# Attention and a mixture of experts on Trainium2: the turn of y split into column halves and moved behind the state's update

## The chip, the cores and the metric

The kernel runs on one core of a Trainium2 chip. Time is the device time of one execution in microseconds (us), the median of three runs. The core's engines work side by side: PE (TensorE: products; a product first loads its weights, 128 rows by up to 128 columns, and then streams columns against them), DVE (VectorE), ACT (ScalarE), POOL (GpSimd) and SP (SyncE, which here only starts transfers). Each engine runs its instructions in the order in which they are written, and waits on semaphores for what the others deliver.

## The reference

```python
gamma = 1.0 - 2.0 ** (-5.0 - np.arange(H))             # B, H, S, D = 4, 8, 768, 64
for t in range(S):
    state = gamma[None, :, None, None] * state + np.einsum('bhd,bhe->bhde', k[:, :, t], v[:, :, t])
    y[:, :, t] = np.einsum('bhd,bhde->bhe', q[:, :, t], state) / np.sqrt(D)
x = y.transpose(0, 2, 1, 3).reshape(B * S, H * D)      # 3072 tokens of 512
noisy = x @ w_gate + np.log1p(np.exp(x @ w_noise)) * noise
top2 = np.argpartition(-noisy, 2, axis=1)[:, :2]       # of 8 experts, softmax over the two
for e in range(8):                                     # F = 1024
    h = np.maximum(x[mask] @ w1[e], 0.0)
    out[mask] += top2_w[mask, k, None] * (h @ w2[e])   # for the tokens that chose e
```

## The kernel before

The program has two parts. The first is the attention, in 24 chunks of 128 tokens, six for each batch (chunk j, c = j % 6 within the batch). Here and below, a tile is named as the rows of the trace name it.

For chunk j, `qk(j)` (L353) multiplies keys and scaled queries into two banks `pA` (16 instructions on 64 rows of the array), and DVE masks them with the decay into `am` (L356). `y_state(j)` (L368) adds queries times the state `U` into `pY`; it is left out for c = 0. `y_mm(j)` adds `am` times the scaled values `vp` (L375), has ACT copy `pY` to `yt` (L379), brings the state up to date in `pU` (L384, left out for c = 5; ACT copies it to `U`, L386), and has ACT square `yt` into `sq` (L388). `x_turn(j)` turns `yt` so that tokens lie on partitions: four f32 products against `turn`, an identity with the gates' weights beside it, give both the turned y and the logits, in `pT` (L401); four one-column products over `sq` (L405) give each token's sum of squares. `x_scale(j)` (L420, L421, DVE) makes a power of two of that, and `x_split(j)` writes x as two f16 parts: ACT the first (L427) and the logits `lgs` (L415), DVE the rest (L431), SP the result to `xbuf` in DRAM (L432).

The loop over j issues, in this order: `qk(j+1)`, `x_turn(j-1)`, `y_state(j)`, steps of the routing (which expert takes which token: `middle`, `mid`, `todo`, `first_todo`), `v_scale(j+1)` and `q_scale(j+2)` on POOL (L326, L334, which make `vp` and `qs` out of loaded `in_v` and `in_q`), `x_scale(j-1)`, `load(j+4)`, `x_split(j-1)`, `y_mm(j)`. Sums of squares of the experts' weights (L207, ACT) are among the steps. Before the loop PE multiplies constants (`busy`, L122, `WARM` of them in two portions around the products L129 and L130, and L821 three times).

The second part is the experts. A block f of expert e is `mm1` (L873 to L875: x and w1 in f16 parts, twelve products into a bank `pH`), `h_hi` (ACT, L879, `hh`) and `h_lo` (DVE, L882, `hl`), and then the second layer in L919 to L921 and L975. Behind the loop stand `p0` to `p7`, the first 384 slots of expert 0, which cover the last turn `x_turn(23)`, its x and the last routing: `mb` (L481) is what the product L492 counts with. L217 is a product for the scale of a weight. In the blocks of expert 0 that follow, counted by n, `tables()` runs at n = 11: `ranked` (L666, L668) and `rows_of` (L634 to L636) make on DVE the table `idx`, by which POOL gathers tokens (L723).

Of the kernel before, what the change touches and what calls it, by code (L numbers as in the profile page):

```python
# [10 lines left out]
F32 = mybir.dt.float32  # L11
F16 = mybir.dt.float16
BF = mybir.dt.bfloat16
# [7 lines left out]
C = 128  # L21
# [39 lines left out]
QW = HP * C + NC * HP  # L61
WARM, BUSY = (4, 3), 3

# [38 lines left out]
def moe_kernel(ctx, tc, qT, kT, kt, vt, noise, wgn, w1, w2, ctab, qtab, xbuf, out):  # L102
# [220 lines left out]
    def v_scale(j):  # L323
        c = j % NC
        VP[j] = loads.tile([128, H, D], F32, name="vp", bufs=2)
        nc.gpsimd.tensor_tensor(VP[j], IN["v", j].rearrange("p (h d) -> p h d", h=H),  # L326
                                vtab[:, c, :, None].to_broadcast([128, H, D]), op=OP.mult)
# [43 lines left out]
    def y_mm(j):  # L371
        c = j % NC
        for i in range(HP):
            for s in range(2):
                nc.tensor.matmul(yplace(j, i, s), VP[j][:, 2 * i + s, :], AM[j][:, s, i, :],  # L375
                                 start=(not c and i < 2), stop=True, skip_group_check=True)
        YT[j] = loads.tile([128, 2, 2, C], F32, name="yt", bufs=2)
        y = YT[j].rearrange("p s g c -> p (s g c)")
        nc.scalar.activation(y.rearrange("p (s x) -> p s x", s=2), PY.pop(j)[:, :, :2 * C], AF.Copy)  # L379
        if c < NC - 1:  # L380
            for i in range(HP):
                for s in range(2):
                    h = 2 * i + s
                    nc.tensor.matmul(pU[s * 64:s * 64 + 64, i, :], IN["kt", j][:, h * 64:h * 64 + 64], VP[j][:, h, :],  # L384
                                     start=(c == 0 and i == 0), stop=True, skip_group_check=True)
            nc.scalar.activation(U[(c + 1) % 2], pU, AF.Copy)  # L386
        SQ[j] = loads.tile([128, KT, C], BF, name="sq", bufs=1)
        nc.scalar.activation(SQ[j].rearrange("p n c -> p (n c)"), y, AF.Square)  # L388

    def x_turn(j):  # L390
# [8 lines left out]
        for s in range(2):  # L399
            for g in range(2):  # L400
                nc.tensor.matmul(p[:, s, g * 128:g * 128 + XW], y[:, s, g, :], turn[:, v, 2 * s + g],  # L401
                                 start=(g == 0), stop=True, skip_group_check=True)
        q = SQ.pop(j)
# [255 lines left out]
    def ranked():  # L659
# [8 lines left out]
        nc.vector.tensor_reduce(tk.rearrange("p (r t) -> p r t", r=m), tp, axis=AX.X, op=OP.add)  # L668
        rows_of(tk, NBLK, NCOL)

# [79 lines left out]
    def P(j, f, *a, d=mid):  # L750
        d.setdefault(j, []).append((f, a))
# [36 lines left out]
    P(23, route_p, 1, d=middle)  # L788
    P(23, route_n, 1)
    P(23, route_g, 1)  # L790
    at(0, turn_gate, 0)
# [30 lines left out]
    for j in range(NCH):  # L822
        if j + 1 < NCH:
            qk(j + 1)
        if j:
            x_turn(j - 1)
        y_state(j)
        for f, a in middle.get(j, []):
# [17 lines left out]
        for f, a in todo.get(j, []):  # L846
            f(*a)
        y_mm(j)
        for f, a in first_todo.get(j, []):
# [12 lines left out]
    def mm1_pe(e, n0, n1, f, between=None):  # L862
        MM[0] += 1
        tag = "pA" if MM[0] % 3 else "pX" if MM[0] > 3 else "pU"
        p = (psum2[0] if tag == "pX" else psum).tile([128, 512], F32, name="pH", tag=tag, bufs=2 if tag == "pA" else 1)
# [140 lines left out]
    x_turn(j)  # L1006
    x_scale(j)
    h_hi(*p0)
    h_lo(*p0)
    x_split(j, lambda: route_x(2, 0, NC))  # L1010
    pctx.close()
# [13 lines left out]
    route_c(2)  # L1025
    w_hi(0, "2", 1)
    h_lo(*p1)
    h_lo(*p2)
# [53 lines left out]

    def tables():
        ranked()
        for _ in range(2):
            ahead.pop(0)()

    for e in range(E):
# [10 lines left out]
        for n0, n1 in cols:  # L1099
# [3 lines left out]
            for f in range(FT):  # L1103
# [33 lines left out]
                if e == 0 and n == 11:  # L1137
                    tables()
                if e == 0 and n == 13:
# [139 lines left out]
```

## Time and profile before

| | |
|---|---|
| runs, us | 646.54, 646.7, 647.61 (median 646.7) |
| profiled execution | 645.92, its span 644.1 |
| PE busy | 634.5 us, 99% |
| DVE, ACT, POOL busy | 287.6 (45%), 300.2 (47%), 204.0 us (32%) |
| mean granted TensorE clock | 0.998 |
| DMA | 113 MB, 175 GB/s |

The span runs from the first to the last instruction of the profiled execution; the device time is longer by what lies around it. Busy shares are means over the whole program. The loop over the chunks takes the first 111 us, the experts the rest.

### The profile page before, as it was taken

The page shows a single profiled execution, that of the slowest core. Times are in us where ns is not written, and L with a number is a line of the kernel's source. Part 1 is how long each engine was busy: PE and PEld are TensorE (multiplying, and loading weights), DVE is VectorE, ACT ScalarE, POOL GpSimd, SP SyncE. Part 2 cuts the span into 40 slices and gives each one's busy share as a digit, 9 for nine tenths or more (in the row PEclk, how much of TensorE's full clock was granted, in tenths as well). Part 3 has the DMA queues.
Part 4 walks back from the last instruction along what each step waited for, and adds up shares of the span by engine and source line. Part 5 has one row for each costly group of instructions (what it writes and reads, how often), then busy time and mean ns, then how long its engine had stood idle before and what let it go on. Part 6 is the DMA issues. An engine that isn't in the chain of part 4 may idle for free.

```text
span 644.1 us, 12255 instructions
## 1 busy us (share of the span) xinstructions
PE 634.5 (99%) x4919; PEld 390.3 (61%) x4919; DVE 287.6 (45%) x740; ACT 300.2 (47%) x559; POOL 204.0 (32%) x166
## 2 busy tenths in 40 slices
PE   9999999999999999999999999999999999999995
PEld 6999998549578544554455445544554465455574
DVE  4678785897454221654162226222622262215020
ACT  6577457615652543554354345434543454344121
POOL 4555472041540134104410433043304430430214
PEclk9999999999999999999999999999999999999999
DMA  8999999978888066845773576447654784483303
GB/s 300 379 386 382 335 319 268 371 188 295 167 139 263 4 130 113 235 99 101 148 191 136 91 137 182 162 82 132 192 161 82 120 211 147 86 118 62 50 10 43
DMA packets 94423, 113.02 MB, mean 175 GB/s; under 512 B 60662, under 2 KB 61820, under 8 KB 90780
## 3 DMA queue, kind: packets, MB, share of 16 engines
q1 hardware_dynamic: 82576, 85.57, 44.2%
q0 software_dynamic: 11776, 26.63, 23.4%
q8 instruction: 40, 0.66, 0.4%
q14 instruction: 19, 0.16, 0.1%
q10 hardware_dynamic: 12, 0.01, 0.0%
HBM read 72.66 MB, written 26.42 MB: 154 GB/s over the span
## 4 chain that ended last, share of the span: by engine, by line
PE 95%; ACT 2%; DVE 1%; issue 1%; POOL 0%; DMA 0%; POOLq 0%; ACTq 0%
PE pH L873 13%; PE pH L875 13%; PE pH L874 13%; PE pO L919 12%; PE pO L921 12%; PE pO L920 12%; PE pA L353 4%; PE pT L401 4%; PE pY L375 4%; PE pT L975 2%; PE pY L368 2%; PE pO L963 2%; PE pU L384 1%; ACT junk L207 1%; PE pO L951 1%; PE pO L949 1%
## 5 line engine op out<-in xcount | busy, mean ns | idle before, releaser
L910 POOL DMA_INDIRECT out<-ot,idx x51 | 82.4, 1616 | 323.2 <-ACT ot L905 181.1
L873 PE MATMUL pH<-xe,w1h 128*128 128x384 f16 (+5 forms) x576 | 180.9, 314 | 0.4 <-DVE hl L882 0.4
L875 PE MATMUL pH<-xe,w1l 128*128 128x384 f16 (+5 forms) x576 | 180.8, 314 | 0.0
L874 PE MATMUL pH<-xe,w1h 128*128 128x384 f16 (+5 forms) x576 | 180.8, 314 | 0.0
L882 DVE SCALAR_TENSOR_TENSOR hl<-pH,hh 128x384 f16<-128x384 f32 (+5 forms) x144 | 75.6, 527 | 140.0 <-ACT hh L879 139.5
L921 PE MATMUL pO<-w2h,hl 128*128 128x512 f16 x344 | 130.4, 379 | 0.0
L920 PE MATMUL pO<-w2l,hh 128*128 128x512 f16 x344 | 130.4, 379 | 0.0
L919 PE MATMUL pO<-w2h,hh 128*128 128x512 f16 x344 | 130.3, 379 | 0.0
L879 ACT ACTIVATE hh<-pH 128x384 f16<-128x384 f32 (+5 forms) x144 | 67.3, 467 | 122.5 <-PE pH L875 111.7
L905 ACT ACTIVATE ot<-pO,gse 128x512 f32<-128x512 f32 x45 | 30.9, 687 | 155.7 <-PE pO L921 139.5
L235 DVE SCALAR_TENSOR_TENSOR w1l<-wst,wsc,w1h 128x1024 f16<-128x1024 f32 x28 | 35.9, 1284 | 95.3 <-ACT w1h L230 95.3
L873 PEld LDWEIGHTS <-w1h 128*128 128x128 f16 x576 | 56.3, 98 | 33.0 <-issue 2.7
L875 PEld LDWEIGHTS <-w1l 128*128 128x128 f16 x576 | 56.3, 98 | 30.9
L874 PEld LDWEIGHTS <-w1h 128*128 128x128 f16 x576 | 56.3, 98 | 30.3 <-issue 0.5
L207 ACT ACTIVATE junk<-wst 128x1024 bf16<-128x1024 f32 x64 | 67.2, 1050 | 0.1
L723 POOL DMA_INDIRECT xg<-xbuf,idx x54 | 57.4, 1062 | 29.0 <-issue 11.9
L921 PEld LDWEIGHTS <-hl 128*128 128x128 f16 x344 | 33.6, 98 | 40.6
L919 PEld LDWEIGHTS <-hh 128*128 128x128 f16 x344 | 33.6, 98 | 40.6 <-issue 0.4
L920 PEld LDWEIGHTS <-hh 128*128 128x128 f16 x344 | 33.6, 98 | 39.6
L356 DVE TENSOR_TENSOR am<-pA,mask 128x512 f32<-128x512 f32 x48 | 30.8, 683 | 17.9 <-PE pA L353 17.9
L326 POOL TENSOR_TENSOR vp<-in_v,cs 128x512 f32<-128x512 f32 x24 | 25.2, 1049 | 36.3 <-issue 16.3
L230 ACT ACTIVATE w2h<-wst,wsc 128x1024 f16<-128x1024 f32 x32 | 36.5, 1140 | 0.2 <-DVE wsc L185 0.2
(181 smaller groups left out, 681.3 us busy)
## 6 DMA issues: line engine op xcount, KB each, us to landing
wst<-w SPq DMA_DIRECT2D x28, 1024.0 KB
in_q<-qT SPq DMA_DIRECT2D x24, 256.0 KB
in_k<-kT SPq DMA_DIRECT2D x24, 256.0 KB
in_v<-vt SPq DMA_DIRECT2D x24, 256.0 KB
in_kt<-kt SPq DMA_DIRECT2D x24, 256.0 KB
xbuf<-x SPq DMA_DIRECT2D x24, 256.0 KB
out<-zero SPq DMA_DIRECT2D x6, 1024.0 KB
wst<-w SPq DMA_DIRECT2D x8, 512.0 KB
```

What stands on the lines that cost most here:

```text
L207: nc.scalar.activation(junk, st[:, i * 1024:(i + 1) * 1024], AF.Square, accum_out=ss[:, i:i + 1])
L230: nc.scalar.activation(hi, st[:, i * 1024:(i + 1) * 1024], AF.Copy, scale=sc[:, 0:1])
L723: nc.gpsimd.indirect_dma_start(out=x[:n], out_offset=None, in_=xbuf[:128 + B0 * S] if e == 0 and t < 3 else xbuf, in_offset=bass.IndirectO ...
L873: nc.tensor.matmul(p[:, :n], whi, xh, start=(k == 0), stop=False)
L874: nc.tensor.matmul(p[:, :n], whi, xl, start=False, stop=False)
L875: nc.tensor.matmul(p[:, :n], wlo, xh, start=False, stop=(k == KT - 1))
L879: nc.scalar.activation(hh[:, f, n0:n1], p, AF.Relu)
L882: nc.vector.scalar_tensor_tensor(hl[:, f, n0:n1], p, 0.0, hh[:, f, n0:n1], op0=OP.max, op1=OP.subtract)
L910: nc.gpsimd.indirect_dma_start(out=out, out_offset=bass.IndirectOffsetOnAxis(ap=idx[:n, i:i + 1], axis=0), in_=ot[:n], in_offset=None, com ...
L919: nc.tensor.matmul(p, a, WT["2h"][:, f, :], start=(f == 0), stop=False)
L920: nc.tensor.matmul(p, a, WT["2l"][:, f, :], start=False, stop=False)
L921: nc.tensor.matmul(p, c, WT["2h"][:, f, :], start=False, stop=(f == FT - 1))
```

## The change

Four things change. In `x_turn` each of the four products becomes two, on 64 columns of weights each, that write the two halves of the partitions. In the loop `x_turn(j-1)` moves behind `y_state(j)` and `y_mm(j)`, which both move up, ahead of the steps of routing; `vp` gets a third buffer and `sq` a second. At the start, five and two constant products stand in place of four and three. Behind the loop, `x_split(23)` comes ahead of `h_hi(p0)`, `h_lo(p0)` moves back to the other `h_lo`, the banks of the `pH` tiles are dealt out in another order, `route_n` and `route_g` of the second group go from ahead of `x_split` to behind it in chunk 23, and `tables` is cut in two: `ranked` at n = 11, `rows_of` at n = 12.

```diff
@@ -59,7 +59,7 @@
 CW = _o
 SOON = _C["vtab"][1]
 QW = HP * C + NC * HP
-WARM, BUSY = (4, 3), 3
+WARM, BUSY = (5, 2), 3
 
 
 def _constants():
@@ -322,7 +322,7 @@
 
     def v_scale(j):
         c = j % NC
-        VP[j] = loads.tile([128, H, D], F32, name="vp", bufs=2)
+        VP[j] = loads.tile([128, H, D], F32, name="vp", bufs=3)
         nc.gpsimd.tensor_tensor(VP[j], IN["v", j].rearrange("p (h d) -> p h d", h=H),
                                 vtab[:, c, :, None].to_broadcast([128, H, D]), op=OP.mult)
 
@@ -384,7 +384,7 @@
                     nc.tensor.matmul(pU[s * 64:s * 64 + 64, i, :], IN["kt", j][:, h * 64:h * 64 + 64], VP[j][:, h, :],
                                      start=(c == 0 and i == 0), stop=True, skip_group_check=True)
             nc.scalar.activation(U[(c + 1) % 2], pU, AF.Copy)
-        SQ[j] = loads.tile([128, KT, C], BF, name="sq", bufs=1)
+        SQ[j] = loads.tile([128, KT, C], BF, name="sq", bufs=2)
         nc.scalar.activation(SQ[j].rearrange("p n c -> p (n c)"), y, AF.Square)
 
     def x_turn(j):
@@ -398,8 +398,9 @@
         y = YT.pop(j)
         for s in range(2):
             for g in range(2):
-                nc.tensor.matmul(p[:, s, g * 128:g * 128 + XW], y[:, s, g, :], turn[:, v, 2 * s + g],
-                                 start=(g == 0), stop=True, skip_group_check=True)
+                for r in (slice(0, 64), slice(64, 128)):
+                    nc.tensor.matmul(p[r, s, g * 128:g * 128 + XW], y[:, s, g, r], turn[:, v, 2 * s + g],
+                                     start=(g == 0), stop=True, skip_group_check=True)
         q = SQ.pop(j)
         for n in range(KT):
             nc.tensor.matmul(PT[j, "s"], q[:, n], oneb[:, 0:1], start=(n == 0), stop=(n == KT - 1), skip_group_check=True)
@@ -666,7 +667,7 @@
         nc.vector.tensor_tensor(tp, v[:, None].to_broadcast(s4), pm[:, :, None, :].to_broadcast(s4), op=OP.mult)
         tk = work.tile([128, NCB], F32, name="tk")
         nc.vector.tensor_reduce(tk.rearrange("p (r t) -> p r t", r=m), tp, axis=AX.X, op=OP.add)
-        rows_of(tk, NBLK, NCOL)
+        return tk
 
     def rank_caps():
         m = E - 1
@@ -786,8 +787,8 @@
     P(22, route_m, 1)
     at0(22, route_c, 1)
     P(23, route_p, 1, d=middle)
-    P(23, route_n, 1)
-    P(23, route_g, 1)
+    at(23, route_n, 1)
+    at(23, route_g, 1)
     at(0, turn_gate, 0)
     at(3, turn_ident, 1)
     at(3, turn_gate, 1)
@@ -822,9 +823,10 @@
     for j in range(NCH):
         if j + 1 < NCH:
             qk(j + 1)
+        y_state(j)
+        y_mm(j)
         if j:
             x_turn(j - 1)
-        y_state(j)
         for f, a in middle.get(j, []):
             f(*a)
         if j < 2:
@@ -845,7 +847,6 @@
             x_split(j - 1)
         for f, a in todo.get(j, []):
             f(*a)
-        y_mm(j)
         for f, a in first_todo.get(j, []):
             f(*a)
     lctx.close()
@@ -861,7 +862,7 @@
 
     def mm1_pe(e, n0, n1, f, between=None):
         MM[0] += 1
-        tag = "pA" if MM[0] % 3 else "pX" if MM[0] > 3 else "pU"
+        tag = "pU" if MM[0] == 3 else "pX" if MM[0] > 3 and MM[0] % 3 == 1 else "pA"
         p = (psum2[0] if tag == "pX" else psum).tile([128, 512], F32, name="pH", tag=tag, bufs=2 if tag == "pA" else 1)
         n = n1 - n0
         for k in range(KT):
@@ -1005,9 +1006,8 @@
         zero_out(i)
     x_turn(j)
     x_scale(j)
+    x_split(j, lambda: route_x(2, 0, NC))
     h_hi(*p0)
-    h_lo(*p0)
-    x_split(j, lambda: route_x(2, 0, NC))
     pctx.close()
     psum2.append(ctx.enter_context(tc.tile_pool(name="psum2", bufs=1, space=bass.MemoryType.PSUM)))
     psum2[0].tile([128, DM], F32, name="pO", tag="pY", bufs=2)
@@ -1024,6 +1024,7 @@
     p3 = first(3, lambda: route_p(2))
     route_c(2)
     w_hi(0, "2", 1)
+    h_lo(*p0)
     h_lo(*p1)
     h_lo(*p2)
     h_hi(*p3)
@@ -1080,8 +1081,8 @@
     for t in range(3):
         put(0, t, made[t])
 
-    def tables():
-        ranked()
+    def tables(tk):
+        rows_of(tk, NBLK, NCOL)
         for _ in range(2):
             ahead.pop(0)()
 
@@ -1135,7 +1136,9 @@
                     flush()
                     out_scale(0, 3, NBLK)
                 if e == 0 and n == 11:
-                    tables()
+                    tk = ranked()
+                if e == 0 and n == 12:
+                    tables(tk)
                 if e == 0 and n == 13:
                     ahead.pop(0)()
                 n += 1
```

PE, one turn of the loop before; the names are tiles, `x8` counts what stands in a row:

```order
L368 MATMUL pY<-qs,U_170 64x128 x8
L375 MATMUL pY<-am,vp 64x128 x8
L384 MATMUL pU<-vp,in_kt 64x64 x8
L353 MATMUL pA<-qs,in_k 128x128 x8
L401 MATMUL pT<-turn,yt 128x144 x4
L405 LDWEIGHTS sq
L405 MATMUL pT<-oneb,sq 128x1
```

And PE in the changed kernel, one turn from its qk on:

```order
L353 MATMUL pA<-qs,in_k 128x128 x8
L368 MATMUL pY<-qs,U_171 64x128 x8
L375 MATMUL pY<-am,vp 64x128 x8
L384 MATMUL pU<-vp,in_kt 64x64 x8
L402 MATMUL pT<-turn,yt 64x144 x8
L406 LDWEIGHTS sq
L406 MATMUL pT<-oneb,sq 128x1
```

The turn stands between update and squares instead of between qk and squares, and qk is followed by the state's products. All lines behind L385 have a number one higher in the changed kernel.

DVE behind the loop, from the scale of the last x on, before (`hl` of 128x384 is `h_lo`, first of p0, then of p1 and p2):

```order
L420 TENSOR_SCALAR p2m<-pT 128x1
L421 TENSOR_SCALAR xsa<-p2m 128x1
L882 SCALAR_TENSOR_TENSOR hl<-pH,hh 128x384
L442 TENSOR_TENSOR lg_1728<-lgs_1729 128x96
L431 SCALAR_TENSOR_TENSOR x_2088<-pT,xsa,x_2088 128x512
...
L481 TENSOR_TENSOR mb_2144<-oh 128x54
L483 TENSOR_TENSOR den_2146<-m_6_2126 128x6
L882 SCALAR_TENSOR_TENSOR hl<-pH,hh 128x384 x2
```

and now:

```order
L421 TENSOR_SCALAR p2m<-pT 128x1
L422 TENSOR_SCALAR xsa<-p2m 128x1
L443 TENSOR_TENSOR lg_1825<-lgs_1826 128x96
L432 SCALAR_TENSOR_TENSOR x_2182<-pT,xsa,x_2182 128x512
...
L482 TENSOR_TENSOR mb_2239<-oh 128x54
L484 TENSOR_TENSOR den_2241<-m_6_2221 128x6
L883 SCALAR_TENSOR_TENSOR hl<-pH,hh 128x384 x3
```

The first `hl` moved from between scale and x to behind `mb`.

DVE at the tables of expert 0, before:

```order
L882 SCALAR_TENSOR_TENSOR hl<-pH,hh 128x192 x4
L666 TENSOR_TENSOR tp<-pB,pm 128x343
L668 TENSOR_REDUCE tk<-tp 128x49
L634 TENSOR_SCALAR roww<-tk,ct 128x49
L635 SCALAR_TENSOR_TENSOR roww<-tk 128x49
L636 SCALAR_TENSOR_TENSOR idx<-roww 128x49
L882 SCALAR_TENSOR_TENSOR hl<-pH,hh 128x192 x4
```

and now:

```order
L667 TENSOR_TENSOR tp<-pB,pm 128x343
L669 TENSOR_REDUCE tk<-tp 128x49
L883 SCALAR_TENSOR_TENSOR hl<-pH,hh 128x192
L635 TENSOR_SCALAR roww<-tk,ct 128x49
L636 SCALAR_TENSOR_TENSOR roww<-tk 128x49
L637 SCALAR_TENSOR_TENSOR idx<-roww 128x49
L883 SCALAR_TENSOR_TENSOR hl<-pH,hh 128x192 x3
```

One `hl` stands between the two halves of the tables.

## Rows read from the trace of the kernel before

**Rows 1.** The page: busy time, share of the span, instructions of each engine.

```profile
PE 634.5 (99%) x4919; PEld 390.3 (61%) x4919; DVE 287.6 (45%) x740; ACT 300.2 (47%) x559; POOL 204.0 (32%) x166
```

**Rows 2.** Waits of PE, 8 to 640 us: total us, times, longest.

```profile
PE pR L492 <- DVE mb L481: 0.6, 1, 0.6
PE pH L873 <- DVE hl L882: 0.4, 1, 0.4
```

**Rows 3.** PE's timeline, one turn: start, us, line, rows*columns, shape, [idle before].

```profile
19.67 1.16 PE L353 MATMUL pA<-qs,in_k 64*128 64x128 f32 x16
20.76 1.25 PE L401 MATMUL pT<-turn,yt 128*128 128x144 f32 x8
21.85 0.24 PE L405 MATMUL pT<-oneb,sq 128*128 128x1 bf16 x4
22.02 0.67 PE L368 MATMUL pY<-qs,U 64*64 64x128 f32 x16
22.62 1.09 PE L375 MATMUL pY<-am,vp 128*64 128x128 f32 x16
23.54 0.64 PE L384 MATMUL pU<-vp,in_kt 128*64 128x64 f32 x16
24.10 1.16 PE L353 MATMUL pA<-qs,in_k 64*128 64x128 f32 x16
```

**Rows 4.** PE's timeline of the same turn products, two windows that cut the group.

```profile
21.23 0.65 PE L401 MATMUL pT<-turn,yt 128*128 128x144 f32 x4
...
21.48 0.53 PE L401 MATMUL pT<-turn,yt 128*128 128x144 f32 x3
```

**Rows 5.** PE's timeline at a change of columns in the experts' second layer.

```profile
178.51 0.38 PE L920 MATMUL pO<-w2l,hh 128*128 128x512 f16 x1
178.72 0.38 PE L921 MATMUL pO<-w2h,hl 128*128 128x512 f16 x1
179.03 0.40 PE L975 MATMUL pT<-w2h,hh 128*64 128x512 f16 x1
```

**Rows 6.** DVE's timeline, iteration 3, from its x on.

```profile
23.38 0.75 DVE L431 SCALAR_TENSOR_TENSOR x<-pT,xsa,x 128x512 f16<-128x512 f32 x1 [0.90 <-ACT lgs L415]
24.04 0.48 DVE L304 COPY turn<-ident 128x256 f32<-128x256 f32 x2
...
25.59 1.22 DVE L356 TENSOR_TENSOR am<-pA,mask 128x512 f32<-128x512 f32 x2
```

**Rows 7.** DVE's timeline, iteration 16.

```profile
78.57 0.26 DVE L535 TENSOR_TENSOR posb<-pR,t 128x108 f32<-128x108 f32 x1
...
80.58 0.74 DVE L431 SCALAR_TENSOR_TENSOR x<-pT,xsa,x 128x512 f16<-128x512 f32 x1
```

**Rows 8.** ACT's timeline, a chunk's copies and square.

```profile
101.42 0.60 ACT L379 ACTIVATE yt<-pY 128x512 f32<-128x512 f32 x1 [0.43 <-PE pY L375]
...
102.18 0.63 ACT L388 ACTIVATE sq<-yt 128x512 bf16<-128x512 f32 x1
```

**Rows 9.** PE's timeline, the loop's last turn of y.

```profile
106.50 1.25 PE L401 MATMUL pT<-turn,yt 128*128 128x144 f32 x8 [0.24 <-ACT yt L379]
```

**Rows 10.** DVE's and PE's timeline behind the loop: `hl` of p0, and L492.

```profile
113.97 0.56 DVE L882 SCALAR_TENSOR_TENSOR hl<-pH,hh 128x384 f16<-128x384 f32 x1 [0.76 <-ACT hh L879]
...
118.40 0.19 PE L492 MATMUL pR<-mb,trib 128*128 128x54 bf16 x1 [0.65 <-DVE mb L481]
```

**Rows 11.** DVE's and PE's timeline at the tables.

```profile
160.91 0.51 DVE L668 TENSOR_REDUCE tk<-tp 128x49 f32<-128x343 f32 x1
...
161.79 0.25 PE L875 MATMUL pH<-xe,w1l 128*128 128x192 f16 x1
...
161.98 0.35 DVE L882 SCALAR_TENSOR_TENSOR hl<-pH,hh 128x192 f16<-128x192 f32 x1
```

**Rows 12.** PE's timeline, the first qk.

```profile
4.78 2.20 PE L353 MATMUL pA<-qs,in_k 64*128 64x128 f32 x16
```

**Rows 13.** POOL's timeline, the queries of chunk 10.

```profile
42.39 1.27 POOL L334 TENSOR_TENSOR qs<-in_q,gq 128x512 f32<-128x512 f32 x1 [0.35 <-DMA in_q<-qT]
```

## The prediction, before the changed kernel ran

> **What bounds the kernel now.** The page's busy times come first: PE is busy for 634.5 of 644.1 us and no other engine for half of it [rows 1]. So the end moves only with PE's own time and with PE's waits. The list of what PE waits for, from the first chunk to the last product, has four lines, 1.4 us in all; the two largest are the 0.6 us of L492 for DVE's `mb` and the 0.4 us of L873 for DVE's `hl` [rows 2]. All else is the spacing of products, so the next view is PE's timeline of one turn of the loop [rows 3]: qk 1.09 us from start to start, turn 1.09, squares 0.17, state 0.60, values (L375) 0.92, state update (L384) 0.56, together 4.43 (24.10 - 19.67).
>
> Why the order of groups matters is in the same rows. The two numbers ahead of a shape such as 64x128 are the rows and columns of the array that a product uses. L353 and L375 both issue sixteen instructions of 128 columns, two side by side; L375, followed by a group of the same form, takes 0.92, L353, followed by another form, 1.09 [rows 3]. A change of form thus costs 0.1 to 0.2 us: the array runs empty and the next weights are not loaded beside a product. That a change of columns alone costs too is seen elsewhere: from L920 to L921, of one form, it is 0.21 from start to start, from L921 to L975, on half the columns, 0.31 [rows 5].
>
> **The change, part by part.** *A, the loop.* Each product of the turn becomes two on 64 columns, the form of L384, and it now follows L384. One instruction of the turn more or less in a cut of its group is 0.12 us (0.65 - 0.53) [rows 4]. Eight of them are 0.98 and the group's 1.09 holds 0.11 for a first load that nothing covers. Two halves on different columns run side by side, as the pairs of L375 do (sixteen instructions of 128 columns in 0.92, or 0.115 a pair) [rows 3], so streaming stays 8 x 0.12. What changes are the borders. Update to turn has no change of form left: 0.56 becomes 0.46. Turn to squares has one now: 7 x 0.12 to the last pair, then 0.21 (the last pair and an emptying array), 1.07 in place of 1.09. Qk to state keeps a change, so qk stays 1.09; squares keep 0.17, state 0.60, values 0.92. The sum is 1.09 + 0.60 + 0.92 + 0.46 + 1.07 + 0.17 = 4.31, a gain of 0.12. The turns of chunks 0 to 21 lie in full turns of the loop: 22 x 0.12 = **-2.64**. The bounds: 0.06 if the border ahead of the squares costs as much as the one behind L353 (-1.3), and 0.18 if it costs nothing beyond the stream (-4.0).
>
> *B, waits inside the loop.* On DVE the mask of the next chunk (`am`, 1.22) stands in the same place of the order, but PE now reaches qk earlier after the squares. `x` of a chunk ends 2.28 us after its squares begin (23.38 + 0.75 - 21.85) [rows 3, 6]. The next qk begins 0.17 after the squares, so x and then the mask are through 2.28 + 1.22 - 0.17 = 3.33 after it, and the qk behind that, which needs the mask's pA back, comes at 4.31: about 0.95 to spare. It is used up where DVE has more behind or ahead of x: in iteration 3 two copies into `turn` hold it for 1.55 (24.04 to 25.59) [rows 6], which costs up to 0.6, and less if the copies shrink beside an idle POOL; I take 0.3. In iteration 16 L535 to L565 stand ahead of x for 2.0 (78.57 to 80.58) [rows 7], about 1.0 more than usual, with two short steps behind: 0.3. On ACT, x now queues behind `yt`, `U` and `sq` of the next chunk. They take 1.39 from the start of the first to the end of the last (101.42 to 102.18 + 0.63) [rows 8]; `yt` is released by L375, whose group ends as the update begins, 0.46 + 1.07 = 1.53 ahead of the squares, so `sq` ends near the squares' start, while x waits for its scale, two DVE steps behind the squares. That is covered except where the sums of squares of weights (L207) fill ACT's queue. **+0.6**, between 0 (copies and steps shrink) and 1.3 (twice the price of these two iterations).
>
> *C, the last turn of the loop.* There is no qk in iteration 23, so behind the squares of chunk 21 only 0.17 + 0.60 + 0.92 = 1.69 pass until the turn of 22 wants `pT` back, which x of 21 releases 2.28 after the squares began: a wait of 0.6 to 0.7, where it waits 0.24 for `yt` now [rows 9]. **+0.4**, between 0 (x there is quicker) and 0.8.
>
> *D, behind the loop.* The chain to the last routing runs from the squares of 23 to L492 at 118.40, and PE waits the last 0.65 of it [rows 2, 10]. `hh` and `hl` of p0 no longer stand ahead of x on ACT and DVE; `hl` is 0.56 [rows 10], and x on ACT comes some 0.4 earlier, as the sums of squares still run ahead of it. **-0.4**, between 0 and -0.65 (the whole wait). Next late is then the weight scale of L217, whose ACT step is not moved. `hl` of p0 holds its bank longer; p3 takes the bank of pX instead, so nobody waits for that one.
>
> *E, the tables.* `ranked` and `rows_of` stood as one block on DVE ahead of an `hl`: tk ends at 161.42, the `hl` for which L873 waits 0.4 [rows 2] begins at 161.98 and ends at 162.33; L875 ahead of it begins at 161.79, and 192 columns stream in 0.08 (192 of 512 at 0.21) [rows 5, 11], so L873 could begin at 161.87. With `rows_of` one block later, `hl` can end at 161.42 + 0.35 = 161.77, ahead of that. **-0.5**; if the wait only moves one block on, 0.
>
> *F, the start.* One warm product moves ahead of L129, one of three behind it goes. The first qk takes 2.20 us, the later ones 1.16 [rows 3, 12]: the same sixteen instructions last nearly twice as long, which I read as the lower of the clock's two levels (1.2 of 2.4 GHz). The same count of columns is streamed, with no pause between L130 and the group behind it. **+0.05**. The bounds are one qk at either level: +1.0 if the raise comes that much later (2.20 - 1.16), -1.0 if it comes ahead of the first.
>
> *Covered.* `vp` with three buffers and `sq` with two take waits off POOL and ACT, on which PE does not wait. The loads of q feed POOL just in time around chunk 10: `qs` is done at 43.66 after POOL waited 0.35 for its DMA [rows 13]. Its qk comes six turns of the loop behind that at 19.67 [rows 3], of which one lacks the update and one the state, near 19.67 + 6 x 4.43 - 0.56 - 0.60 = 45.1, less 6 x 0.12 = 0.7 by A: some 0.7 us is left. `gates_out` and the last x go out on SP's queue some 2 us later; the first gathers wait for the tables of indices, not for them.
>
> The sum: -2.64 + 0.6 + 0.4 - 0.4 - 0.5 + 0.05 = -2.5. The profiled execution, 645.92 us with a span of 644.1, becomes 643.4; the median of the runs lies 0.8 above it, so 646.7 becomes **644.2**. With the bounds of A and B and half of the others' it is 643.2 to 645.1 for this case alone.
>
> **The rivals.** *Slower: x on ACT.* If `yt`, `U` and `sq` hold ACT so long that x starts 1.2 later in each iteration, the 3.33 above becomes 4.53, PE waits 0.22 in each of 22, and 4.8 comes on: with B's 0.6 inside it, 648.4. It decides from 0.95 of delay. For it: the three take 1.39, more than that. Against: L375 and L384 now release them ahead of the turn. 0.07.
>
> *Slower: each instruction costs.* The turn has eight instructions more. The four one-column products of the squares take 0.17 with their border, so at most 0.04 each [rows 3]; were that paid for each, 8 x 0.04 x 23 = 7.4, or 651.6. Against: L375's sixteen cost no more than eight pairs, 0.115 each for 128 columns. If halves did not run side by side at all, 8 x 0.12 x 23 = 22 would come on. 0.05 for both. The Trainium skill, in TensorEngine Tiling (Array Packing), under Instruction Overhead, says that each matmul has an overhead of about 60 cycles and warns against taking the tiling from a dimension that is small; 60 cycles at 2.4 GHz would be 0.025 us, the spacing of the squares. By that rule the estimate is 8 x 0.025 x 23 = 4.6 more, 648.8; by the pairs of L375 it is 644.2, and the trace agrees with those.
>
> *Faster: a change of columns costs little.* If the border ahead of the squares and that between qk and state came cheaper by 0.09 and 0.1 each turn, 22 x 0.19 = 4.2 more would go: 640.0. Against: L975's 0.31 [rows 5]. 0.06.
>
> *The gain is given back.* The loop turns faster, but `am` waits in more iterations than two (B at 1.3), the wait of D or E only moves, or the clock comes later: 645.7, within measurement of before. 0.20.
>
> **How the numbers follow.** The forecast has 0.62, the rivals 0.07, 0.05, 0.06 and 0.20. About 0.2%, 1.3 us, is what a measurement of this kernel can tell: faster is below 645.4, slower above 648.0. Of the forecast 0.58 is faster, with the 0.06 and a third of the last rival 0.71; the same 0.18; slower 0.11. For 8 in 10 the range leaves out the fast rival and the two slow ones, and takes in most of the last: 642.7 to 646.1.
>
> **What would show it.** A: from qk to qk 4.31 in most iterations, the turn directly 0.46 behind the update, squares 1.07 behind the turn's start. 4.43 or more with no wait would put A wrong, and a spacing above 0.12 in the turn the pairs. B: waits of L353 for `am`, in iterations 3 and 16 alone. C: one wait of the first turn behind the loop's last values for x. D and E: L492's wait at 0.2 or so, L873's gone. F: the first qk still 2.20, the next group at full clock. The prediction is wrong if L353 waits in each iteration, or if L353 at its start in iteration 3 stands later than 19.67 - 2 x 0.12.

## The result, and the profile after

The changed kernel takes 654.04 us (median of four runs, 652.24 to 654.89), the kernel before 646.62 beside it: a ratio of 1.0113, interval 1.0099 to 1.0127. It is 7.4 us slower where 2.5 us less was forecast, and it lies outside the range of 642.7 to 646.1. The profiled execution took 653.44 us.

The page's busy times of the changed kernel, which answer to [rows 1]: PE is busy for 1.2 us more, and the span is 7.4 us longer.

```profile
PE 635.7 (98%) x5111; PEld 387.6 (59%) x5111; DVE 295.3 (45%) x740; ACT 299.0 (46%) x559; POOL 205.1 (31%) x166
```

DVE has 7.7 us more of busy time with the same 740 instructions: some of them last longer. PE's waits from 8 to 645 us (total us, times, longest), which answer to [rows 2], without two lines of 0.2 us:

```profile
PE pT L402 <- DVE x L432: 2.2, 4, 0.9
PE pY L368 <- ACT U L386: 1.7, 1, 1.7
PE pA L353 <- POOL qs L334: 1.5, 4, 0.9
PE pT L402 <- DVE cum L547: 0.5, 1, 0.5
PE pH L874 <- DVE hl L883: 0.3, 1, 0.3
PE pY L375 <- POOL vp L326: 0.3, 1, 0.3
```

Four lines became eight, and the large new ones lie in the loop: the turn waits for x to leave `pT`, the state for `U`, qk for `qs` (of these 1.5 us, 0.95 are a wait for the mask, as is shown below). `cum` is DVE's step directly behind an x, so that its line too is the turn waiting for x. Between them an undisturbed turn of the loop on PE's timeline, which answers to [rows 3]:

```profile
19.30 1.16 PE L353 MATMUL pA<-qs,in_k 64*128 64x128 f32 x16
20.39 0.67 PE L368 MATMUL pY<-qs,U 64*64 64x128 f32 x16
20.98 1.09 PE L375 MATMUL pY<-am,vp 128*64 128x128 f32 x16
21.91 0.64 PE L384 MATMUL pU<-vp,in_kt 128*64 128x64 f32 x16
22.37 1.15 PE L402 MATMUL pT<-turn,yt 128*64 128x144 f32 x16
23.46 0.25 PE L406 MATMUL pT<-oneb,sq 128*128 128x1 bf16 x4
23.64 1.16 PE L353 MATMUL pA<-qs,in_k 64*128 64x128 f32 x16
```

It takes 23.64 - 19.30 = 4.34 in place of 4.43, and the forecast had 4.31. So PE's own work is nearly as forecast, and the waits are not. Where the time went, by starts on PE's timeline (us; the third qk began at 10.80 before and at 10.40 after, so 0.40 was won ahead of the table):

| kernel | third to last qk | last qk to last squares | last squares to last product |
|---|---|---|---|
| before | 90.96 | 10.83 | 524.06 |
| changed | 96.16 | 13.93 | 523.58 |
| e1_loop | 95.75 | 13.17 | 523.54 |
| e2_rest | 90.95 | 10.83 | 523.09 |
| e4_move | 97.93 | 14.25 | 523.51 |
| e9_vp3 | 100.20 | 10.84 | 524.04 |
| e14_nopool_before | 92.97 | 10.83 | 524.04 |
| e15_nopool_after | 93.52 | 12.33 | 523.44 |
| e18_gate2 | 93.17 | 16.32 | 523.85 |
| e19_gate2_defer | 92.03 | 13.10 | 524.68 |

-0.40 + 5.20 + 3.10 - 0.48 = 7.4. Each row is one profiled execution.

**What a wait looks like.** Before, the step that makes `vp` of chunk 12, the one that makes `qs` of chunk 13, and the weights' remainder L242 (engine timelines of POOL and DVE of the kernel before):

```profile
54.41 1.04 POOL L326 TENSOR_TENSOR vp<-in_v,cs 128x512 f32<-128x512 f32 x1 [2.26 <-PE pU L384]
55.41 1.28 POOL L334 TENSOR_TENSOR qs<-in_q,gq 128x512 f32<-128x512 f32 x1
56.91 1.40 DVE L242 SCALAR_TENSOR_TENSOR w1l<-wst,wsc,w1h 128x512 f16<-128x512 f32 x2
```

POOL waits 2.26 for the update, computes from 54.41 to 56.69, and is silent when DVE begins its two steps, 1.40 for both. In the changed kernel, same steps, with x and the turn that waits for it:

```profile
54.66 2.42 DVE L242 SCALAR_TENSOR_TENSOR w1l<-wst,wsc,w1h 128x512 f16<-128x512 f32 x2
55.19 1.35 POOL L334 TENSOR_TENSOR qs<-in_q,gq 128x512 f32<-128x512 f32 x1 [0.93 <-DMA in_q<-qT]
...
57.01 0.74 DVE L432 SCALAR_TENSOR_TENSOR x<-pT,xsa,x 128x512 f16<-128x512 f32 x1
...
57.89 1.20 PE L402 MATMUL pT<-turn,yt 128*64 128x144 f32 x16 [0.72 <-DVE x L432]
```

POOL's qs lies inside L242, which lasts 1.02 longer; x is late by that, and the turn waits 0.72. The clearest case is a short step, the sum of the logits, 0.249 us in the kernel before. In the changed kernel (POOL and DVE timeline):

```profile
91.97 1.15 POOL L724 DMA_INDIRECT xg<-xbuf,idx  x1 [4.63 <-DMA xbuf<-x]
92.59 2.96 DVE L443 TENSOR_TENSOR lg<-lgs 128x96 f32<-128x96 f32 x1
93.15 1.05 POOL L326 TENSOR_TENSOR vp<-in_v,cs 128x512 f32<-128x512 f32 x1
94.16 1.26 POOL L334 TENSOR_TENSOR qs<-in_q,gq 128x512 f32<-128x512 f32 x1
95.47 1.27 DVE L356 TENSOR_TENSOR am<-pA,mask 128x512 f32<-128x512 f32 x2
...
96.25 1.71 PE L353 MATMUL pA<-qs,in_k 64*128 64x128 f32 x16 [0.95 <-POOL qs L334]
```

It stands for 2.96 us, until POOL's row of steps ends at 95.42, and with it the mask behind it. The qk at 96.25 waits for that mask: the list puts its 0.95 down to `qs`, but `qs` had ended at 95.42, and the first of the mask's two steps ends near 96.1. Steps that read PSUM do not stretch: the mask's mean is 676 ns after and 683 before, that of x 745 and 747 (grouped lines, 16 to 110 us). Steps with a single input can stretch: four copies into `turn`, L304's two and L311's two, before and then after:

```profile
24.04 0.48 DVE L304 COPY turn<-ident 128x256 f32<-128x256 f32 x2
24.32 1.11 POOL L326 TENSOR_TENSOR vp<-in_v,cs 128x512 f32<-128x512 f32 x1 [2.15 <-PE pU L384]
24.44 1.11 DVE L311 COPY turn<-wgf 128x32 f32<-128x32 f32 x2
```

```profile
25.61 1.04 POOL L326 TENSOR_TENSOR vp<-in_v,cs 128x512 f32<-128x512 f32 x1
25.66 1.34 DVE L304 COPY turn<-ident 128x256 f32<-128x256 f32 x2
26.92 0.26 DVE L311 COPY turn<-wgf 128x32 f32<-128x32 f32 x2
```

Each pair is long where POOL computes beside it, and short where it does not.

### The profile page after: what moved, and what is told of

The parts are those of the page before. It is cut to its first block, busy times and chain, and to the rows that moved or that the text cites. A ratio compares the mean times of both kernels' runs of the same rounds, so it can differ in the third digit from the quotient of the medians.

```text
span 651.5 us, 12650 instructions
## 1 busy us (share of the span) xinstructions
PE 635.7 (98%) x5111; PEld 387.6 (59%) x5111; DVE 295.3 (45%) x740; ACT 299.0 (46%) x559; POOL 205.1 (31%) x166
## 4 chain that ended last, share of the span: by engine, by line
PE 84%; DMA 8%; DVE 4%; ACT 1%; issue 1%; POOL 1%; SPq 1%; POOLq 0%; ACTq 0%
PE pH L874 12%; PE pH L875 12%; PE pH L876 12%; PE pO L920 11%; PE pO L922 11%; PE pO L921 11%; DMA wst<-w 3%; PE pT L402 2%; DMA in_q<-qT 2%; PE pT L976 2%; PE pO L964 2%; PE pY L375 2%; PE pA L353 1%; DMA in_k<-kT 1%; DVE w1l L242 1%
## 5 line engine op out<-in xcount | busy, mean ns | idle before, releaser
L874 PE MATMUL pH<-xe,w1h 128*128 128x384 f16 (+5 forms) x576 | 180.9, 314 | 0.3 <-DVE hl L883 0.3
L235 DVE SCALAR_TENSOR_TENSOR w1l<-wst,wsc,w1h 128x1024 f16<-128x1024 f32 x28 | 36.0, 1285 | 96.1 <-ACT w1h L230 92.2
L874 PEld LDWEIGHTS <-w1h 128*128 128x128 f16 x576 | 56.3, 98 | 32.8 <-issue 2.5
L207 ACT ACTIVATE junk<-wst 128x1024 bf16<-128x1024 f32 x64 | 67.2, 1049 | 6.2 <-DMA wst<-w 6.1
L724 POOL DMA_INDIRECT xg<-xbuf,idx x54 | 57.0, 1055 | 40.5 <-issue 12.5
L334 POOL TENSOR_TENSOR qs<-in_q,gq 128x512 f32<-128x512 f32 (+1 forms) x24 | 30.6, 1276 | 34.2 <-DMA in_q<-qT 21.3
L230 ACT ACTIVATE w1h<-wst,wsc 128x1024 f16<-128x1024 f32 x32 | 36.1, 1139 | 1.3 <-DVE wsc L185 1.3
```

What stands on the lines that cost most here:

```text
L207: nc.scalar.activation(junk, st[:, i * 1024:(i + 1) * 1024], AF.Square, accum_out=ss[:, i:i + 1])
L230: nc.scalar.activation(hi, st[:, i * 1024:(i + 1) * 1024], AF.Copy, scale=sc[:, 0:1])
L724: nc.gpsimd.indirect_dma_start(out=x[:n], out_offset=None, in_=xbuf[:128 + B0 * S] if e == 0 and t < 3 else xbuf, in_offset=bass.IndirectO ...
L874: nc.tensor.matmul(p[:, :n], whi, xh, start=(k == 0), stop=False)
```

## The experiments

**The parts.** Four kernels split the change: the loop alone, the rest alone, and of the loop the halves alone and the move alone.

```diff
 e1_loop = before, and:       e3_halves: only the second line; e4_move: all but it
+vp bufs=3, sq bufs=2
+for r in (slice(0, 64), slice(64, 128)): matmul(p[r, ...], y[:, s, g, r], ...)
+qk(j + 1); y_state(j); y_mm(j); x_turn(j - 1)
 e2_rest = changed kernel without these
```

> The loop's change alone (halves of the turn, the turn behind the update, vp in three buffers, sq in two); start, end, route_n and tables as before. Theory L (the turn's later place makes x late, and x holds pT, ACT's and SP's queue, so the loop loses more by waits than its borders give): 653 to 656, the loss of the whole change and about 1 us that the end gives back. Theory R (the loss comes from the rest: start, banks, the end): 644 to 646. Theory S (transfers bound the loop, a faster PE only waits): 646 to 647.

> All but the loop's change: start of 5 and 2 warm products, route_n and route_g of chunk 23 behind x, x ahead of hh of p0, banks, tables in two steps. The turn stands whole at its old place. Theory L and S: 645.3 to 646.3, the prediction's D and E of -0.9 and the start's +0.05. Theory R: 651 to 654.

> The halves alone, the turn at its old place between qk and squares. Five changes of form per turn of the loop in place of four: if halves run side by side and a change ahead of the squares costs 0.08, 22 x 0.08 = 1.8 more, 648; if the change costs nothing, 646.6. All theories agree here; it measures the border. If halves did not run side by side, 668.

> The move alone: the whole turn behind the update, buffers as in the changed kernel, the rest as before. PE's own groups are then as long as before (4.43). Theory L: 653 to 657, as x is as late as in the changed kernel. Theory S: 646.5 to 647. Theory R: 646.5.

Measured beside a median of 646.34: e1_loop 654.38, ratio 1.0126 (1.0109 to 1.0143); e2_rest 645.13, 0.9981 (0.9971 to 0.9990); e3_halves 648.66, 1.0027 (1.0014 to 1.0041); e4_move 656.91, 1.0161 (1.0134 to 1.0187). The loss is the loop's alone. The rest wins 1.2 us. The halves at the old place cost 1 to 2.5 us, one change of form more in each turn (4.49 from qk to qk for 4.43); in the new place they win 656.91 - 654.38 = 2.5, near what step A said, though the runs of each kernel lie up to 3 us apart. The move with its buffers, without the halves, costs 10.6.

**One buffer.** The change gives vp a third buffer, which the prediction held for free.

```diff
 before
-        VP[j] = loads.tile([128, H, D], F32, name="vp", bufs=2)
+        VP[j] = loads.tile([128, H, D], F32, name="vp", bufs=3)
```

> The kernel before, with vp in three buffers in place of two and nothing else: POOL no longer waits for the state's update (11.9 us in 7 waits), and so runs earlier. The prediction had this at nothing. Theory P: L242 longer than 1.4, x later, 647.5 to 650. Without P: 646.3 to 646.9.

655.58 us, ratio 1.0126 (1.0075 to 1.0176): this buffer alone, in the old order, costs as much as the whole change. Its DVE, POOL and PE timelines:

```profile
97.86 3.16 DVE L242 SCALAR_TENSOR_TENSOR w1l<-wst,wsc,w1h 128x512 f16<-128x512 f32 x2
...
98.53 1.27 POOL L334 TENSOR_TENSOR qs<-in_q,gq 128x512 f32<-128x512 f32 x1
...
100.95 0.74 DVE L431 SCALAR_TENSOR_TENSOR x<-pT,xsa,x 128x512 f16<-128x512 f32 x1
...
101.83 1.57 PE L401 MATMUL pT<-turn,yt 128*128 128x144 f32 x8 [2.91 <-DVE x L431]
...
103.42 1.13 PE L368 MATMUL pY<-qs,U 64*64 64x128 f32 x16
```

POOL now runs ahead and falls on L242, which lasts 3.16; x is late and the turn waits 2.91. Two more turns wait, 1.12 at 73.39 and 1.85 at 84.81, and ahead of their x too stand stretched steps: `oh`, L478, lasts 1.30 (0.38 before), L556 1.26 (0.17) and L565 1.84 (1.09). So the wait of POOL for the update, 11.9 us in seven waits before, was no loss: it held POOL to the part of the turn in which DVE reads PSUM or rests. Not all of the price is waiting. The three waits are 5.9 of the 9.2 us that the loop loses in the table; behind the two longer ones PE's own products last longer (above, L368 1.13 for 0.67), at a mean granted clock of 0.61 from 84.81 to 89.19 and 0.60 from 101.83 to 106.11, part of it at 1.2 of the 2.4 GHz. Beside the same products of the kernel before, that makes 1.5 us each time.

The reverse does not mend the changed kernel:

```diff
 changed kernel
-bufs=3  (vp)
+bufs=2
```

> The changed kernel with vp in two buffers, as before. There v_scale(j+1) stands behind y_mm(j), so its buffer is free one update earlier and nothing holds POOL. If the third buffer alone is the cause in the changed kernel too: 645 to 647. If POOL is let loose by the new order as much as by the buffer: 653 to 655.

652.91, 1.0101 (1.0078 to 1.0124), near the changed kernel's 654.04, as I expected, but not for the reason that I gave. POOL is held there: its list of waits has 7.7 us in six waits for the update. L242's eight steps still last 1155 ns each, for 1219 in the changed kernel and 796 before. In the new order the update stands ahead of the turn and not ahead of qk, so POOL is let go earlier against DVE's steps; and twice its `qs`, late for a load, runs beside L242 (from 54.99 and from 59.89). Which of these weighs more no run tells. Move and buffer each bring POOL onto DVE's steps.

**The queues.** x also became late on SP's queue, where its write stands ahead of the next loads. From 0 to 125 us SP waits eight times for DVE's x before, 7.3 us in all, and fourteen times in the changed kernel, 17.8 us.

e5 issues the write a turn later, e6 holds POOL by its buffers, e7 does both.

```diff
 e5_defer: changed kernel, x16 bufs=4, and
-            nc.sync.dma_start(xbuf[...], x)        # in x_split
+            WQ.append((xbuf[...], x))              # and behind load(j + AHEAD): x_write()
 e6_pool: changed kernel, qs bufs=2, and
+            q_scale(j + 2)
             v_scale(j + 1)
-            q_scale(j + 2)
```

> The changed kernel, but SP issues the write of x one iteration later, behind the next loads (x16 in four buffers), so no load stands in SP's queue behind a late x. Theory Q (late x holds SP's queue, so queries arrive late): waits of qk for qs (1.9 us) and of ACT for wst go, 650 to 652. Theory P (POOL runs at another phase, beside DVE's steps in SBUF, which then take 2.4 in place of 1.4): 653 to 655, the waits for pT stay.

> The changed kernel, but POOL held back to where DVE reads PSUM: qs in two buffers in place of three, so that q_scale(j+2) waits for y_state(j), and v_scale(j+1) behind it. Theory P: L242 back at 1.4 to 1.6 for its two, waits of the turn for pT (2.2 to 4.4 us) mostly gone, 649 to 651. Theory Q: 653 to 655.

> Both of the two former. If P and Q are both right and add up: 645 to 648, and the prediction's 644.2 nearly reached. If neither is the cause: 653 to 655.

652.28, ratio 1.0085 (1.0060 to 1.0109); 652.05, 1.0079 (1.0058 to 1.0099); 651.49, 1.0079 (1.0048 to 1.0109). By the medians each takes some 2 us back, and they do not add up; the intervals overlap or touch the changed kernel's (1.0099 to 1.0127), so little of it is clear of the noise. In their profiles the gain lies at the loop's end, which takes 11.3 us in e5 and 12.5 in e6 for 13.9; from third to last qk they need 96.5 both, no less than the changed kernel. In e6 L242's eight steps fall from 1219 ns to 870 (796 before), but where POOL is released in front of a longer row of DVE's steps it falls on those: L566's two last 1757 ns each for 954, and the turn still waits 1.6, at `cum`.

**POOL held in other ways.** e10 and e11 hold POOL by vp's buffer, e12 adds the write of e5.

```diff
 e10_vp1: changed kernel
-bufs=3  (vp)
+bufs=1
 e11_phase: besides, qs bufs=2 and q_scale(j + 2) ahead of v_scale(j + 1), behind it where c is 0
 e12_phase_defer: e11_phase and the write of e5_defer
```

> The changed kernel with vp in one buffer in place of three: v_scale(j+1) waits for the update of chunk j, so POOL's two steps (1.04 + 1.27) begin as the turn begins and end about 1.3 after the squares begin. Theory P (DVE's steps in SBUF stand still while POOL computes): POOL is off DVE's steps for most of their time, 649 to 651, with L242's pair below 2.0. Theory Q alone (SP's queue): 653 to 654, since the order on SP is the changed kernel's.

> The changed kernel with POOL held on both steps: qs in two buffers and first (it waits for y_state of chunk j), vp in one buffer behind it (it waits for the update of chunk j); where c is 0, vp first. POOL then works from about 2.0 to 4.3 us behind the squares, while DVE does x and am out of PSUM. Theory P: 646 to 649, most waits for pT gone. Q alone: 653 to 654.

> The former, and SP's write of x one iteration later as in e5_defer. P with Q as a smaller second cause: 644.5 to 647, at or below the kernel before. P without Q: as e11_phase.

670.92, ratio 1.0373 (1.0348 to 1.0399); 653.29, 1.0103 (1.0082 to 1.0124); 653.80, 1.0101 (1.0077 to 1.0125). e10 tells nothing of the collision, since I had counted a turn too many: qk(j+2) comes directly behind the squares, before POOL is through, and waits for `qs` 19 times from 8 to 126 us, 23.9 us in all.

In e11 L242 is back at 817 ns a step, but 3.4 us of such waits, made by the experiment where c is 0, and 1.6 at `cum` come in. The same error of counting spoiled the next pair, where POOL stands behind a copy out of x:

```diff
 e16_gate: changed kernel; q_scale and v_scale moved behind x_split(j - 1), ahead of them
+                nc.gpsimd.tensor_copy(held, x16_of[j - 1][:, 1, :1])
 e17_gate_defer: e16_gate and the write of e5_defer
```

> The changed kernel, but POOL's two steps stand behind a one-column copy out of the second part of x, so that they begin only when DVE's steps in SBUF and x are through; q first. Theory P: L242's pair at 1.4, 646 to 650. Otherwise 653 to 655. It may also lose by queries that come too late: q ends about 4.0 us behind the squares, where the next qk is due at 4.5.

> The former, and SP's write of x one iteration later as in e5_defer. If the late write on SP's queue is a second cause: 644.5 to 648, 1 to 3 us under e16_gate. Otherwise as e16_gate.

766.84, 1.1859 (1.1838 to 1.1880), and 767.0, 1.1857 (1.1836 to 1.1878): qk waits 3.6 to 4.3 us for its queries in each turn, and most of these qk then last 2.08 in place of 1.16. e18 and e19 make them one chunk further ahead.

```diff
 e18_gate2: e16_gate, but
-                q_scale(j + 2); v_scale(j + 1)
+                q_scale(j + 3); v_scale(j + 2)
 e19_gate2_defer: e18_gate2 and the write of e5_defer
```

> The changed kernel, POOL's two steps held behind x(j-1) by a one-column copy out of it, as in e16_gate, but made one chunk further ahead (q of chunk j+3, v of j+2), so that no product waits for them at once. POOL then computes from about 2.8 to 5.2 us behind the squares. Theory P: L242's pair at 1.4 to 1.6, the waits of POOL's making (about 6 of the 10 us in the loop) gone, 646.5 to 650. If P is wrong: 652 to 655.

> The former, and SP's write of x one iteration later, behind the next loads, as in e5_defer. Queries are needed earlier there, so the loads matter more: 1 to 2 us under e18_gate2, 645 to 648. If the late write costs nothing: as e18_gate2.

652.66, ratio 1.0094 (1.0078 to 1.0111), and 650.73, 1.0075 (1.0058 to 1.0091). The loop went part of the way and the end did not. POOL is off most of DVE's steps (grouped lines, then timeline of e18_gate2; `held` is the copy):

```profile
L242 DVE SCALAR_TENSOR_TENSOR w1l<-wst,wsc,w1h 128x512 f16<-128x512 f32 x8 | 6.8, 884 | 0.0
...
92.70 0.25 DVE L447 TENSOR_TENSOR lg<-lgs 128x96 f32<-128x96 f32 x1
...
92.91 0.19 POOL L850 COPY held<-x 128x1 f16<-128x1 f16 x1 [1.30 <-DVE x L436]
...
93.05 1.29 POOL L334 TENSOR_TENSOR qs<-in_q,gq 128x512 f32<-128x512 f32 x1
```

The logits' sum is 0.25 again, and the stretch from third to last qk falls from 96.16 to 93.17, with the earlier loads to 92.03 (the table above): half of the 6 us that I had put down to POOL there. In e18 the end then loses 2.4 more: the state waits 3.11 for `U`, as it does for 1.69 in the paragraph on the loop's end, and the products behind it run at a granted clock of 0.50. Of the kernels in which POOL is held off DVE's steps, e6, e11, e18 and e19, none came into the range that I had named for it; e19, the best of them, is 4.3 us above the kernel before.

**Without POOL's work.** The last pair takes POOL's scaling out, in the old order and in the new, so that the products work on unscaled q and v. It also scales the logits by 0.001 and changes buffers: one more for the loaded values, two more for the queries, two in all for the first `vp` and `qs`.

```diff
 e14_nopool_before = before, e15_nopool_after = changed kernel, and in both
+        if j > 1: VP[j] = IN["v", j]; return       # v_scale
+        if j > 1: QS[j] = IN["q", j]; return       # q_scale
-        bufs=AHEAD + {"k": 0, "q": -1, "v": 0, "kt": 1}[n]
+        bufs=AHEAD + {"k": 0, "q": 1, "v": 1, "kt": 1}[n]
```

> The kernel before without POOL's scaling of q and v from chunk 2 on: the loaded tiles go to the products as they are (their buffers one more; the logits are scaled down to stay finite). It is the base for the next run. If POOL bounds nothing in the order before: 645.5 to 646.5.

> The changed kernel without POOL's scaling of q and v in the same way. Theory P (the whole loss is DVE's steps standing still beside POOL, and what follows from a late x): 2.5 to 4 us under the former run, 642 to 644. Theory Q/K (the late x itself, in SP's and ACT's queue, costs as well): 1 to 5 us above the former run.

648.36, ratio 1.0030 (1.0019 to 1.0041), and 650.26, 1.0064 (1.0046 to 1.0082). The base is itself 2 us slower than before: its loop has stalls near 92 us, when POOL gathers, for which I have no cause. e15 has them as well (a turn of 6.15 there, 1.8 too long), so that they nearly cancel. Between the two the change costs 1.9 us in place of 7.4, so POOL's work makes some 5.5 us of the loss, with the waits for `qs` in it, and a rest is there without it. In both L242 takes 744 ns a step and the logits' sum 0.25. What the rest is, e15's waits of PE show (8 to 126 us, the four largest):

```profile
PE pY L374 <- ACT U L392: 1.7, 2, 1.2
PE pT L408 <- issue: 0.7, 3, 0.3
PE pT L408 <- DVE x L438: 0.7, 2, 0.4
PE pT L408 <- DVE cum L553: 0.5, 1, 0.5
```

**The end of the loop.** From last qk to last squares the changed kernel loses 3.1 us. Its timelines of ACT and PE:

```profile
110.70 1.06 ACT L207 ACTIVATE junk<-wst 128x1024 bf16<-128x1024 f32 x1 [2.83 <-DMA wst<-w]
...
111.76 0.58 ACT L379 ACTIVATE yt<-pY 128x512 f32<-128x512 f32 x1
112.24 0.37 ACT L386 ACTIVATE U<-pU 128x256 f32<-128x256 f32 x1
...
112.66 0.67 PE L368 MATMUL pY<-qs,U 64*64 64x128 f32 x16 [1.69 <-ACT U L386]
...
113.26 1.84 PE L375 MATMUL pY<-am,vp 128*64 128x128 f32 x16
...
114.88 2.12 PE L402 MATMUL pT<-turn,yt 128*64 128x144 f32 x16
```

ACT's sum of squares waits 2.83 for its weights, and `yt` and `U` stand behind it; before, L207 waited 0.1 in all. PE is idle for 1.69, and then L375 and L402 last nearly twice as long: the mean granted clock from 112.6 to 117 is 0.61 in the trace's windows, that is partly at 1.2 of the 2.4 GHz, and 1.00 on both sides. From start to start the values take 1.62 in place of 0.92 and the turn 2.06 in place of 1.09, 1.7 us together. In e1_loop, with a wait of 1.5, the turn behind it kept its speed. With the loads earlier (e5) this stretch is 11.3, and the wait for `U` is gone.

## Why the prediction was wrong

**A, right.** 4.34 from qk to qk for 4.31; update to turn 0.46 as said, turn to squares 1.09 for 1.07, squares to qk 0.18 for 0.17. That is a gain of 0.09 a turn, 2.0 us in 22 turns for the 2.64 of the sum; e4_move less e1_loop is 2.5. Halves run side by side: sixteen instructions take the 1.09 that eight took, so that the second rival's 0.04 us an instruction does not show.

**Covered, wrong, and this decided.** "`vp` with three buffers ... take waits off POOL ..., on which PE does not wait" is true, and the step failed at what those waits did: they kept POOL off DVE's steps in SBUF. The price is 9.2 us in the old order (e9_vp3; 4.8 to 11.4 by its interval), of which some 3 are products at the lower clock behind the waits. In the new order it is about 5.5 by the pair without POOL's work; holding POOL behind x gave back 3.0 us of the loop (e18_gate2). The pair without POOL's work does not part the two ways in which POOL can cost here, its steps beside DVE's and late queries that pass through it. The profile before showed both halves, POOL's 11.9 us of waits for L384 and copies on DVE that lasted longer beside POOL; I used the second for iteration 3 alone. There the 1.55 are four copies, not two, and in the changed kernel they did not shrink: they took 25.66 to 27.18, since POOL stood beside the other pair.

The Trainium skill, in SBUF — State Buffer, under "SBUF: two separate sides", says that DVE and GpSimd share one pair of ports under an exclusive lock, that a DVE instruction in a two-port mode or with two inputs in SBUF needs it, and that "the other fully blocks". The trace agrees: `lg`, L242 and L566 have two inputs in SBUF and stretch, the copies L304 and L311 have one and stretch too, `am` and x read PSUM and do not. I had not weighed this rule for the buffer.

**B, wrong by its size and its place.** The waits for the mask inside qk come to 0.50 + 0.10 + 0.14 + 0.55 = 1.3 us, the upper bound, and with the 0.95 ahead of the qk at 96.25 to 2.2. The turn's own wait for x was costed in C alone. In the loop it came to 0.9, 0.1, 0.5, 0.7, 0.5 and 1.0 in six turns: there are only 3.26 us from squares to the next turn (2.79 where c is 5 and the update is missing, 2.66 where c is 0 and the state is), and x needs 2.28 and whatever stands ahead of it on DVE. Even with no POOL the three turns of c = 5 wait 0.5 to 0.65 each (e15_nopool_after). Neither of the two signs named for a wrong prediction came: L353 does not wait in each iteration, and in iteration 3 it starts at 19.30. Both look at L353, and the loss was at the turn.

**C, wrong by its size.** 3.1 us for 0.4. The wait for `pT` shows where nothing else delays the turn: from the values to the turn it is 0.72 longer in e5_defer and 0.54 in e15. In the changed kernel no such wait is listed; the same 0.70 is there L375 at the lower clock. What came in its place, 1.7 for `U` and 1.7 for the clock behind it, was not in the sum. The failed step is the sentence that ACT's queue is "covered except where the sums of squares ... fill" it: they did not fill it, one waited for a transfer, which SP had issued late behind x.

**D, right, E, right without the rest.** In e2_rest L492 waits 0.2 for the 0.65 of before, and L873's wait is gone; the stretch behind the last squares is 0.97 shorter for the 0.9 forecast. In the changed kernel D holds (0.2), but L874 waits 0.3 as L873 did: there ACT's `hh`, behind a sum of squares that waits 0.48 for its weights, is late, not `rows_of`.

**F, right as far as the profiles tell.** Executions with the new start differ, first the changed kernel's, then e2_rest's:

```profile
4.58 1.16 PE L353 MATMUL pA<-qs,in_k 64*128 64x128 f32 x16
```

```profile
4.64 2.08 PE L353 MATMUL pA<-qs,in_k 64*128 64x128 f32 x16
```

By the third qk the one is 0.4 ahead of before and the other 0.8 behind. Of the 14 profiles with the new start, 12 have a first qk of 2.08 and two one of 1.16, and the third qk begins at 10.40 to 11.56, median 10.9; in the six with the old start the first qk takes 2.15 to 2.20 and the third begins at 10.80 to 11.46, median 11.0. So the start is worth about nothing, as the +0.05 had it, and the 0.40 of the changed kernel's profile is luck. That the long qk ran at the lower clock is not shown: the trace's granted clock reads 1.00 from 4.78 to 6.90 before and from 4.64 to 6.60 in e2_rest.

**The transfers.** "Some 0.7 us is left" for the queries failed: qk waits for `qs` in three turns from the one at 40.69 on, 0.16, 0.24 and 0.15 us. x holds SP's queue there: with the write issued later (e5) the three waits are gone. I moved x past ACT's steps and looked at the queue of SP only for the loop's end.

**The rivals.** The slower one named a late x as the mechanism, and x is late. It was tied to ACT's three steps and to the mask's bank, had 0.07, and gave 648.4; what made x late is DVE beside POOL, what waits first is `pT`, and the queues carry it on. The measured 654 lies beyond every time that a rival was given, since none had two engines that slow each other. Nor does the span of 643.2 to 645.1 follow from its bounds: added up as described they give about 641.4 to 647.4. That is a slip of the sum, and 654 lies outside either.

## To carry to other kernels

A wait of an engine that is off the path may be what keeps it out of another engine's way: before a buffer is added that takes it off, look at what runs beside that engine then. Steps whose duration differs between places of the same trace (here 1.40 and 1.83 for the same pair) say that two engines meet, and the sum must carry the longer one. When a step is moved within a loop, follow its result through every queue that carries it, each at its own margin, down to the transfers behind it. Of this change the part outside the loop, e2_rest, beats both kernels: 645.13 us, 0.9981 of before (0.9971 to 0.9990).

## What the runs showed of the hardware

DVE steps that read no PSUM can stand still while POOL computes: 0.249 became 2.96 for 96 columns, across a row of three POOL instructions (a gather, vp, qs). It is not only those with two inputs: the copies L304, with one, went from 284 ns each to 708, and L556, 128x12 with one input, from 0.17 to 1.26 in e9_vp3 beside `qs`; the one-column L422 kept its 0.15. DVE did not get its turn between two POOL steps in that row of three, but it did in e9_vp3, where L565 lasted 1.84 and the `qs` behind it then 1.99 in place of 1.27: POOL waited in its turn.

A change of columns ahead of one-column products was cheap: turn to squares took 1.09 now, with the change, and 1.09 before, without it but with a first load of the turn that nothing covered. By A's estimate of 0.98 for the stream, the change is 0.11 there, against 0.17 behind L353.

Idle times of PE of 1.69 (the changed kernel), 1.85 and 2.91 (e9_vp3) and 3.11 (e18_gate2) were followed by 4 to 6 us in which the mean granted clock was 0.50 to 0.61; one of 2.62 (e4_move) and one of 1.45 (e1_loop), ahead of the same products, were not. So a wait can cost 1.5 us and more beyond its own length, and its length alone does not tell whether it will.
